# Chunked attention with a capacity-limited router: the first pair read with its zeros, one key chain for the last eight row tiles, other one-hot groups, earlier weights

## The chip, the core and the metric

The kernel runs on one NeuronCore of a Trainium2 chip. A core has five instruction streams that run side by side and meet in semaphores: TensorE (PE: matmuls; its weight loads are shown apart as PEld), VectorE (DVE), ScalarE (ACT), GpSimd (POOL) and SyncE (SP, which here only issues DMAs). Sixteen DMA engines move data between the chip's memory and the core's SBUF. They are fed from queues, of which three matter here: SP's, ACT's, and POOL's for gathers and scatters by index. The metric is device time in microseconds (us), the median over runs: 246.68 us for the kernel before (three runs, 246.67 to 246.94).

## What is computed

Attention in chunks of 64 positions is followed by a mixture of eight experts, of which each token uses the one with the largest logit, and each expert keeps at most `capacity` (80) tokens, those with the largest gate weights:

```python
scores = scale * q_c @ k_c.T                 # per chunk of 64, 8 x 8 heads x 9 chunks
attn = exp(scores - max); attn /= attn.sum() + 1e-09
x = (attn @ v_c) as [4608, 512]
logits = x @ w_gate                           # [4608, 8]
expert_idx = argmax(logits);  gate_w = softmax(logits)[expert_idx]
for e in range(8):
    tok = the (at most capacity) tokens of e with the largest gate_w
    out[tok] = gate_w[tok] * (relu(x[tok] @ w1[e]) @ w2[e])     # all other rows of out are 0
```

All data is float32: q, k and v of 8 x 8 heads x 576 x 64, w1 of 8 x 512 x 1024, w2 of 8 x 1024 x 512.

## The kernel before

**Pairs.** The attention runs over 18 pairs of row tiles (a row tile is 128 of the 4608 rows; 36 of them). Pair `n` needs its queries and keys in one of three buffers `qb` (`load_qk`, L320) and its values in one of three buffers `vb` (`load_v`, L328), each load in two DMAs of 64 partitions. In `qb` two of three column blocks are half zeros, so that one matmul makes the scores of two heads; those zeros are set once, at the start, by six DVE memsets (L637, L638), and the buffer's loads wait for them. `scores` (L338) fills PSUM, DVE subtracts the maxima (L348, L353), PE transposes (L363), ACT takes the exponential (L372), `values` (L391) multiplies with v, DVE divides (L406), `store` writes x to memory (`xs`, L419, L414), and PE transposes x for the router's logits (L443, L453). The loop is skewed: in turn `n` stand the scores of `n`, the transposes of x of `n-3`, the values of `n-2` and the exponentials of `n-1`. Every order here is written out by hand: each engine runs its instructions in the order of the code, and SP issues DMAs in the order of the code, each when its semaphores allow.

**Gate chains.** For each group of four row tiles `gate` computes level, one-hot of the expert (`mine`), the gate weight `g = 1 / sum` (L519, L521), the key (L483) and its split into three bfloat16 parts `comp` (L489 to L496) on POOL. Groups 28 and 32 come last, when all pairs are done.

**Routing.** `tally` counts on PE how many tokens lie above each of 256 levels, `left_add` (L568) and `threshold` (L574, L577, L580) find each expert's level, `mask` (L786) marks the candidates, a scan (L791) and three matmuls (L796) give each candidate its place, `ptok` (L802, L804). `hot` makes one-hot matrices of the places, 128 x 128 for each row tile, by DVE for several tiles at once (way "v", L588, at most HOT tiles in an instruction), by ACT (way "a", L598, L599) or by POOL (way "p", L601). 36 matmuls (L813) in the written order `order` collect the candidates' `comp` into `cand`. Then PE spreads the eight experts' keys (L848), DVE ranks them (L831, L837), PE places the chosen rows (L147), and POOL gathers their x from `xs` (L176). `keep_warm` (L610) issues matmuls of 256 columns whose result nobody reads.

**Experts.** Six blocks of 128 slots run layer 1 (L201) and layer 2 (L234). The weights come in 2 MB DMAs (L897) on SP's queue; those of experts 0 and 1 are cut into 16 pieces of 512 KB (`early_weights`, L629) and issued in the last turns by the table EARLY (keys 15 to 17 are loop turns, 18 to 21 places behind the loop). Some of them wait for a tiny POOL copy (L628) into the target tile. The later weights wait until the first gathers have landed (L896) or a buffer comes free; the rows of `out` that no token fills are cleared by DMAs from a zero tile (L616).

Of the kernel before, what the change touches and what calls it, by code (L numbers as in the profile page):

```python
# [8 lines left out]
F32 = mybir.dt.float32  # L9
BF16 = mybir.dt.bfloat16  # L10
# [25 lines left out]
LG = NT - 1  # L36
HOT = 8
OB = 171
LATER = [[(2, 1), (3, 0), (3, 1)], [(0, 2), (4, 0), (5, 0), (1, 2)], [(4, 1), (5, 1), (2, 2)], [(6, 0), (6, 1), (3, 2), (4, 2), (7, 0)], [(7, 1), (5, 2), (6, 2), (7, 2), (8, 2)], [], [], []]

EARLY = {15: [0], 16: [1, 2], 17: [3, 4], 18: [5, 6, 7], 19: [8, 9], 20: [10, 11], 21: [12, 13, 14, 15]}

# [11 lines left out]
@with_exitstack  # L54
def attention_moe(ctx: ExitStack, tc: tile.TileContext, qk, vv, wg, w1, w2, cap, cst, out):
    nc = tc.nc
# [224 lines left out]
    with ExitStack() as actx:  # L281
# [43 lines left out]

        def load_v(n):
            for h in range(2):
                nc.sync.dma_start(vbufs[n % NB][h:P:2, :, h],  # L328
                                  vv[n, :, h].rearrange("t p f -> p t f"))
# [126 lines left out]
        def gate(rt, n, lg, queue):  # L456
# [6 lines left out]
            def t2(nm):  # L463
                return gk.tile([P, n], F32, name=f"{nm}{rt}", tag=nm, bufs=3)
            sh, ex, wt, r = (t3(x) for x in ("sh", "ex", "wt", "r"))
            m, mw, sx, g, u8, lb = (t2(x) for x in ("gm", "mw", "sx", "gg", "u8", "lb"))
            bb = gk.tile([P, n], BF16, name=f"bb{rt}", tag="bb", bufs=3)
            kk, co = keys[:, sl, :], comp[:, sl]
            oh = mine[:, sl, :]
# [12 lines left out]
            def key():  # L482
                nc.gpsimd.tensor_tensor(kk, oh, g[:, :, None].to_broadcast(bc), op=ALU.mult)  # L483
                parts()

            def parts():
                p = nc.gpsimd
                for j, c0 in ((0, C_A), (1, C_B)):
                    p.tensor_tensor(  # L489
                        co[:, :, j, :], oh,  # L490
                        ct[:, c0 + rt:c0 + rt + n, None].to_broadcast(bc), op=ALU.mult)
                p.tensor_copy(co[:, :, 2, :], kk)
                p.tensor_tensor(r, kk, co[:, :, 2, :], op=ALU.subtract)
                p.tensor_copy(co[:, :, 3, :], r)
                p.tensor_tensor(r, r, co[:, :, 3, :], op=ALU.subtract)
                p.tensor_copy(co[:, :, 4, :], r)  # L496

            def level():
                with nc.allow_low_precision(reason="the same level is used everywhere"):
# [20 lines left out]
                        g, sx, 1e-9, None, op0=ALU.add)]  # L520
            late = [lambda: v.reciprocal(g, g), key]  # L521
            for fn in chain + ([] if rt >= 24 else rest + late):
# [59 lines left out]
        def hot(rt, way, n):  # L582

            if way == "v":
                if 'hot' not in S:
                    S['hot'] = wk.tile([P, 5, P, HOT], BF16, name="pk", tag="qb2", bufs=1), deque(range(5))
                oh = S['hot'][0][:, S['hot'][1].popleft()]
# [45 lines left out]
        with tc.manual_schedule():  # L633
            warm = gk.tile([P, 2 * P], BF16, name="warm", tag="lv", bufs=LV)
            nc.gpsimd.memset(warm, 0.0)
            for j, qb in enumerate(qbufs):
                nc.vector.memset(qb[:, :, 0:512], 0.0)  # L637
                nc.vector.memset(qb[:, :, 1024:1536], 0.0)  # L638
                if j == 0:
                    load_qk(0, (nc.sync, nc.scalar))  # L640
            nc.scalar.dma_start(ident, cst[:, C_ID:C_ID + P])
            for j, vb in enumerate(vbufs):
                (nc.vector, nc.gpsimd, nc.gpsimd)[j].memset(vb, 0.0)
            nc.vector.memset(wgp[:, :, 8:32], 0.0)
            pw = bank([P, 256])

# [9 lines left out]
            nc.scalar.mul(idp, ident, float(P))  # L656
            load_qk(1)
            load_qk(2)
            load_v(0)
            load_v(1)  # L660

            def late_constants():
# [106 lines left out]
            for j in range(33, 36):  # L769
                steps_(nc.vector, j)  # L770
            for k in EARLY[20]:
                early_weights(k, bo[:, 28:29])
            for k in EARLY[21]:
                early_weights(k, bo[:, 32:33])
            tally(28, 4)
            left_add(28)
            tally(32, 4)
            rest(28, "level", "sum")
            rest(32, "sum")
            rest(28, "inverse", "key")  # L780
            rest(32, "inverse", "key")
            keep_warm(1)
            threshold()
# [21 lines left out]
            cand = two[:, 1, 0:5 * NE].rearrange("p (c e) -> p c e", c=5)  # L805
            for rt, way in ((31, "p"), (32, "a"), (33, "a"), (34, "a"), (35, "p")):
                hot(rt, way, 1)
            for b0, n in ((0, 5), (5, 8), (13, 8), (21, 6), (27, 4)):
                hot(b0, "v", n)
            order = [*range(0, 13), 32, *range(13, 21), 33, 31, *range(21, 27), 34, 35,  # L810
                     *range(27, 31)]
            for j, rt in enumerate(order):
# [3 lines left out]
                    start=j == 0, stop=j == RT - 1)  # L816
                if rt in (4, 12, 20, 35):
                    keep_warm(1)
# [208 lines left out]
def _arrays(q, k, v, moe_w_gate, moe_w1, moe_w2, moe_capacity):  # L1027
# [7 lines left out]
    r["qk"] = np.ascontiguousarray(np.concatenate(  # L1035
        [np.where(f, k, q), np.where(f, q, k)], -1).reshape(NPAIR, 2, P, QK))
    r["vv"] = np.ascontiguousarray(t.reshape(NPAIR, 2, 2, 64, VW))
    r["wg"] = np.ascontiguousarray(moe_w_gate)
# [22 lines left out]
```

## Time and profile before

| | us |
|---|---|
| median of 3 runs | 246.68 |
| profiled execution | 246.04 |
| its span | 244.2 |
| PE busy | 224.2 (92%) |
| DVE / ACT / POOL busy | 119.1 / 65.8 / 56.6 |

The profile is of one execution, and its span is what its instructions cover. "Idle before, releaser" says how long an engine stood still ahead of an instruction and what ended that. PE's busy time contains the `keep_warm` matmuls, so a busy PE is not always one that the end waits for.

### The profile page before, as it was taken

The numbers are of one execution on the slowest core, as the hardware profiler recorded it, in microseconds if no ns is written. First come the engines' busy times: TensorE is split into PE (matmuls) and PEld (weight loads), VectorE is DVE, ScalarE is ACT, GpSimd is POOL, SyncE is SP. The second block draws the span as 40 slices with busy tenths as digits, with TensorE's granted clock in tenths as the row PEclk, the third lists the DMA queues.
The fourth block names the chain that finished last, engine by engine and source line by source line (L and its number), as shares of the span: only waits on it lengthen the run. The fifth ranks groups of instructions, "written<-read, shape, count | busy, mean of one in ns | idle before, by whom it ended". The sixth has DMA issues, their size and how long they took to land.

```text
span 244.2 us, 7221 instructions
## 1 busy us (share of the span) xinstructions
PE 224.2 (92%) x3121; PEld 143.5 (59%) x3121; DVE 119.1 (49%) x257; ACT 65.8 (27%) x115; POOL 56.6 (23%) x168
## 2 busy tenths in 40 slices
PE   8797799999999999989768979999999999999980
PEld 5587788898898989868547723434234223233320
DVE  7886668696968787877474721112111112111210
ACT  2013433372737364544622011202002002010000
POOL 8000300222222222328685370000000000000271
PEclk9999999999999999999987899999999999999998
DMA  4999999999999996889999979999999999999141
GB/s 127 407 359 337 411 409 406 407 408 404 389 370 349 374 359 219 293 293 300 280 410 410 366 213 400 401 395 415 414 400 409 416 409 415 403 400 403 71 164 61
DMA packets 34741, 84.71 MB, mean 347 GB/s; under 512 B 3024, under 2 KB 3152, under 8 KB 34704
## 3 DMA queue, kind: packets, MB, share of 16 engines
q1 hardware_dynamic: 33456, 80.72, 87.9%
q0 software_dynamic: 960, 2.88, 3.4%
q8 instruction: 26, 0.43, 0.7%
q10 hardware_dynamic: 288, 0.59, 0.6%
q14 instruction: 11, 0.09, 0.1%
HBM read 64.00 MB, written 20.45 MB: 346 GB/s over the span
## 4 chain that ended last, share of the span: by engine, by line
PE 70%; DMA 14%; SPq 5%; DVE 3%; POOL 3%; issue 2%; ACT 1%; POOLq 0%; DVEq 0%; ACTq 0%
PE o L391 13%; PE hc L201 13%; PE s L338 13%; PE yc L234 11%; DMA w<-in_w 7%; PE px L363 5%; DMA qb<-in_qk 5%; SPq L616 4%; PE pt L363 4%; PE small L443 4%; PE hpc L219 2%; DMA xgc<-xs,gic 2%; PE small L453 1%; PE pwarm L610 1%; PE xpc L189 1%
## 5 line engine op out<-in xcount | busy, mean ns | idle before, releaser
L201 PE MATMUL hc<-w,xtc 128*32 128x512 f32 x384 | 45.5, 594 | 0.5 <-ACT xtc L191 0.2
L234 PE MATMUL yc<-w,htc 128*32 128x512 f32 x384 | 42.3, 592 | 0.0
L338 PE MATMUL s<-qb 128*64 128x128 f32 x576 | 35.4, 276 | 4.4 <-DMA qb<-in_qk 3.2
L391 PE MATMUL o<-vb,pT 128*64 128x130 f32 x576 | 36.1, 276 | 0.0
L338 PEld LDWEIGHTS s<-qb 128*64 128x64 f32 x576 | 31.2, 137 | 7.2 <-DVE x L406 2.4
L391 PEld LDWEIGHTS o<-vb,pT 128*64 128x64 f32 x576 | 31.5, 135 | 1.2
L234 PEld LDWEIGHTS yc<-w,htc 128*32 128x32 f32 x384 | 12.4, 110 | 28.3 <-issue 28.3
L348 DVE TENSOR_REDUCE mx<-s 128x16 f32<-128x1024 f32 x18 | 22.0, 1225 | 14.1 <-PE s L338 14.0
L201 PEld LDWEIGHTS hc<-w,xtc 128*32 128x32 f32 x384 | 12.0, 110 | 28.2 <-issue 25.6
L372 ACT ACTIVATE pT<-pt 128x1024 f32<-128x1024 f32 x18 | 18.4, 1024 | 31.8 <-PE pt L363 31.8
L253 POOL DMA_INDIRECT out<-ysc,to x6 | 5.9, 991 | 86.6 <-SPq L912 84.4
L434 ACT COPY xT<-px 128x1024 f32<-128x1024 f32 x17 | 17.1, 1008 | 25.3 <-PE px L363 25.3
L406 DVE TENSOR_TENSOR x<-o,rc 128x1024 f32<-128x1024 f32 (+1 forms) x20 | 22.4, 1118 | 0.7
L353 DVE TENSOR_TENSOR sm<-s,mx 128x1024 f32<-128x1024 f32 x18 | 22.1, 1227 | 0.6
L206 ACT ACTIVATE hsc<-hc 128x512 f32<-128x512 f32 x6 | 3.6, 598 | 65.7 <-PE hc L201 65.7
L239 DVE TENSOR_SCALAR ysc<-yc,gatec 128x512 f32<-128x512 f32 x6 | 4.5, 752 | 33.5 <-PE yc L234 33.5
L223 DVE COPY htc<-hpc 128x512 f32<-128x512 f32 x6 | 4.2, 692 | 24.3 <-PE hpc L219 24.3
L208 DVE TENSOR_SCALAR hsc<-hc 128x512 f32<-128x512 f32 x6 | 4.1, 692 | 23.8 <-PE hc L201 23.8
L363 PE MATMUL pt<-ct,sm 64*128 64x64 f32 x288 | 12.8, 229 | 1.2 <-ACT pT L372 1.2
L363 PEld LDWEIGHTS pt<-ct,sm 64*128 64x128 f32 x288 | 10.4, 139 | 4.3 <-issue 2.8
L363 PE MATMUL px<-ct,x 64*128 64x64 f32 x288 | 12.8, 229 | 0.0
L533 ACT ACTIVATE lv<-io_b,bo 128x256 bf16<-128x256 bf16 x29 | 12.5, 498 | 0.4 <-DVE bo L514 0.4
(131 smaller groups left out, 216.5 us busy)
## 6 DMA issues: line engine op xcount, KB each, us to landing
w<-in_w SPq DMA_DIRECT2D x12, 2048.0 KB, 18.2
qb<-in_qk SPq DMA_DIRECT2D x35, 512.0 KB, 6.6
vb<-in_vv SPq DMA_DIRECT2D x36, 260.0 KB, 5.3
out<-zero SPq DMA_DIRECT2D x9, 1024.0 KB, 16.7
xs<-x SPq DMA_DIRECT2D x16, 512.0 KB, 6.2
w<-in_w SPq DMA_DIRECT2D x16, 512.0 KB, 7.1
xs<-x SPq DMA_DIRECT2D x4, 256.0 KB, 5.5
qb<-in_qk ACTq DMA_DIRECT2D x1, 512.0 KB, 4.3
```

What stands on the lines that cost most here:

```text
L201: nc.tensor.matmul(h[o:o + 32, :], lhsT=xT[r][:, b, o:o + 32], rhs=getw(groups[r][g])[0][:, b, 512 * f:512 * f + 512], start=(b == 0), sto ...
L234: nc.tensor.matmul(y[o:o + 32, :], lhsT=hT[r][c // 4][:, c % 4, o:o + 32], rhs=getw(groups[r][g])[1][:, c, :], start=(c == 0), stop=(c == ...
L338: nc.tensor.matmul(ps[64 * u:64 * u + 64, t, P * pr:P * pr + P].rearrange("p (h k) -> p h k", h=2), lhsT=t8[:, 1, pr, u, :], rhs=t8[:, 0:3 ...
L348: nc.vector.tensor_reduce(d['mx'], d['s8'], axis=AX.X, op=ALU.max)
L353: nc.vector.tensor_tensor(d['sm'].rearrange("p c k h -> p h c k"), d['s8'], d['mx'][:, :, :, None].to_broadcast([P, 2, 8, 64]), op=ALU.sub ...
L363: nc.tensor.transpose(pm[:, u, 64 * c:64 * c + 64], src(c)[rows], ident[rows, rows])
L372: nc.scalar.activation(d['pT'], pt, AF.Exp, scale=0.125)
L391: nc.tensor.matmul(po[64 * u:64 * u + 64, o:o + 130].rearrange("p (h x) -> p h x", h=2), lhsT=d['pT'][:, u, c:c + 64], rhs=v[:, :, pr, u, ...
L406: nc.vector.tensor_tensor(TT[T][:, r:r + nt, :].rearrange("p r (k h e) -> p (r k) h e", k=4, h=2), pov[..., 0:64], rc[:, :, :, None].to_br ...
L434: nc.scalar.copy(dst, pm)
L443: nc.tensor.matmul(pl[32 * j:32 * j + 32], lhsT=wgp[:, pr], rhs=xt[:, 4 * (j % 2) + pr, :], start=pr == 0, stop=pr == 3, tile_position=(0, ...
L533: nc.scalar.activation(lv, io_b, AF.Sign, bias=bo[:, rt:rt + 1], scale=-1.0)
```

## The change

The host lays out the first pair's queries and keys a second time with the zeros already in them (`qk0`, two blocks of 128 x 1536 float32); two DMAs, one of SP and one of ACT, read it with no memset ahead of them. Buffer 1's zeros stay on DVE, buffer 2's go to POOL, and the loads of pairs 1 and 2 and of values 0 and 1 are shared between SP's and ACT's queues. Groups 28 and 32 keep their sums in one tile `g8`, with one reciprocal and one key chain of eight row tiles where there were two of four. The DVE one-hots are made in three instructions (12, 12 and 6 row tiles) where there were five (5, 8, 8, 6 and 4); POOL makes those of 30 and 31, ACT those of 32 to 35. `keep_warm` calls move, and EARLY issues the pieces one place sooner, with two POOL copies in front of them where there were six.

```diff
@@ constants
-HOT = 8
+HOT = 12
-EARLY = {15: [0], 16: [1, 2], 17: [3, 4], 18: [5, 6, 7], 19: [8, 9], 20: [10, 11], 21: [12, 13, 14, 15]}
+EARLY = {15: [0, 1], 16: [2, 3], 17: [4, 5], 18: [6, 7, 8], 19: [9, 10, 11], 20: [12, 13], 21: [14, 15]}
@@ load_v
-        def load_v(n):
+        def load_v(n, engs=(nc.sync, nc.sync)):
             for h in range(2):
-                nc.sync.dma_start(vbufs[n % NB][h:P:2, :, h],
+                engs[h].dma_start(vbufs[n % NB][h:P:2, :, h],
@@ gate
-            m, mw, sx, g, u8, lb = (t2(x) for x in ("gm", "mw", "sx", "gg", "u8", "lb"))
+            m, mw, sx, u8, lb = (t2(x) for x in ("gm", "mw", "sx", "u8", "lb"))
+            if rt < 28:
+                g = t2("gg")
+            else:
+                if rt == 28:
+                    S['g8'] = gk.tile([P, 8], F32, name="g8", tag="g8", bufs=1)
+                g = S['g8'][:, rt - 28:rt - 24]
...
             def key():
-                nc.gpsimd.tensor_tensor(kk, oh, g[:, :, None].to_broadcast(bc), op=ALU.mult)
-                parts()
-
-            def parts():
-                p = nc.gpsimd
+                if rt == 32:
+                    keyed(28, 8, S['g8'], gk.tile([P, 8, NE], F32, name="r8", tag="r8", bufs=1))
+                elif rt < 28:
+                    keyed(rt, n, g, r)
+
+            def keyed(rt, n, g, r):
+                p, bc = nc.gpsimd, [P, n, NE]
+                kk, co, oh = keys[:, rt:rt + n], comp[:, rt:rt + n], mine[:, rt:rt + n]
+                p.tensor_tensor(kk, oh, g[:, :, None].to_broadcast(bc), op=ALU.mult)
...
-            late = [lambda: v.reciprocal(g, g), key]
+            late = [lambda: v.reciprocal(S['g8'] if rt == 32 else g, S['g8'] if rt == 32 else g)
+                    if rt != 28 else None, key]
@@ hot
-                    S['hot'] = wk.tile([P, 5, P, HOT], BF16, name="pk", tag="qb2", bufs=1), deque(range(5))
+                    S['hot'] = wk.tile([P, 3, P, HOT], BF16, name="pk", tag="qb2", bufs=1), deque(range(3))
@@ the start
-            for j, qb in enumerate(qbufs):
-                nc.vector.memset(qb[:, :, 0:512], 0.0)
-                nc.vector.memset(qb[:, :, 1024:1536], 0.0)
-                if j == 0:
-                    load_qk(0, (nc.sync, nc.scalar))
+            for t, eng in enumerate((nc.sync, nc.scalar)):
+                eng.dma_start(qbufs[0][:, t], qk0[t])
             nc.scalar.dma_start(ident, cst[:, C_ID:C_ID + P])
+            for j, eng in ((1, nc.vector), (2, nc.gpsimd)):
+                eng.memset(qbufs[j][:, :, 0:512], 0.0)
+                eng.memset(qbufs[j][:, :, 1024:1536], 0.0)
...
+            both = (nc.sync, nc.scalar)
+            load_qk(1, both)
+            load_qk(2, both)
+            load_v(0, both)
+            load_v(1, both)
...
-            load_qk(1)
-            load_qk(2)
-            load_v(0)
-            load_v(1)
@@ after the pairs
-            for k in EARLY[20]:
-                early_weights(k, bo[:, 28:29])
-            for k in EARLY[21]:
-                early_weights(k, bo[:, 32:33])
+            for j in (20, 21):
+                for k in EARLY[j]:
+                    early_weights(k, bo[:, 4 * j - 52:4 * j - 51] if k == EARLY[j][0] else None)
             tally(28, 4)
             left_add(28)
+            keep_warm(4)
             tally(32, 4)
             rest(28, "level", "sum")
             rest(32, "sum")
-            rest(28, "inverse", "key")
             rest(32, "inverse", "key")
-            keep_warm(1)
+            keep_warm(4)
             threshold()
...
-            for rt, way in ((31, "p"), (32, "a"), (33, "a"), (34, "a"), (35, "p")):
+            for rt, way in ((30, "p"), (31, "p"), (32, "a"), (33, "a"), (34, "a"), (35, "a")):
                 hot(rt, way, 1)
-            for b0, n in ((0, 5), (5, 8), (13, 8), (21, 6), (27, 4)):
+            for b0, n in ((0, 12), (12, 12), (24, 6)):
                 hot(b0, "v", n)
-            order = [*range(0, 13), 32, *range(13, 21), 33, 31, *range(21, 27), 34, 35,
-                     *range(27, 31)]
+            order = [*range(0, 12), 32, *range(12, 24), 33, 30, 34, *range(24, 30), 31, 35]
...
-                if rt in (4, 12, 20, 35):
+                if rt in (32, 34):
                     keep_warm(1)
@@ _arrays
+    a = r["qk"][0].reshape(2, 2, 64, QK)
+    z = np.zeros((2, 64, 2, QK + 512), a.dtype)
+    z[:, :, 0, :QK], z[:, :, 1, 512:] = a[:, 0], a[:, 1]
+    r["qk0"] = z.reshape(2, P, QK + 512)
```

On SP, at the start of the program, with what each row waits for (`qb_99` to `qb_101` are the three buffers of queries and keys, `vb_102` and `vb_103` two of values; DVE_49 and Pool_49 are semaphores of those engines, DMAHW those of DMAs). Before:

```order
L320 DMA qb_99<-in_qk 64x2x1024 [waits DVE_49]
L320 DMA qb_100<-in_qk 64x2x1024 [waits DVE_49] x2
L320 DMA qb_101<-in_qk 64x2x1024 [waits DVE_49] x2
L328 DMA vb_102<-in_vv 64x2x520 [waits DVE_49]
L328 DMA vb_102<-in_vv 64x2x520 [waits DMAHW0_49]
```

The same place on SP in the change:

```order
L647 DMA qb_99<-in_qk 128x1536
L320 DMA qb_100<-in_qk 64x2x1024 [waits DVE_49]
L320 DMA qb_101<-in_qk 64x2x1024 [waits Pool_49]
L328 DMA vb_102<-in_vv 64x2x520 [waits DVE_49]
L328 DMA vb_103<-in_vv 64x2x520 [waits DMAHW1_49,Pool_49]
```

The first load no longer waits for DVE and is half as large again; of each later pair one half stays on SP, and the other half stands on ACT.

On POOL, behind the key chain of group 24 (`gg` are the sums of a group, `w` targets of weights, `r` what a key has left after a part is taken off). Before, up to the middle of the second of two chains:

```order
L628 COPY w_1_2197<-bo 128x1 x2
L628 COPY w_1_2198<-bo 128x1 x4
L516 TENSOR_TENSOR kb<-mine,bb_2212 128x4x8
L519 TENSOR_SCALAR gg_2209<-sx_2208 128x4
L519 TENSOR_SCALAR gg_2276<-sx_2275 128x4
L483 TENSOR_TENSOR keys<-mine,gg_2209 128x32
L489 TENSOR_TENSOR comp<-mine,ct 128x4x8 x2
L492 CAST comp<-keys 128x4x8
L493 TENSOR_TENSOR r_2205<-keys,comp 128x32
L494 CAST comp<-r_2205 128x4x8
L495 TENSOR_TENSOR r_2205<-r_2205,comp 128x32
L496 CAST comp<-r_2205 128x4x8
```

The same place on POOL in the change:

```order
L638 COPY w_1_2140<-bo 128x1 x2
L525 TENSOR_TENSOR kb<-mine,bb_2212 128x4x8
L528 TENSOR_SCALAR g_2211<-sx_2208 128x4
L528 TENSOR_SCALAR g_2211<-sx_2275 128x4
L496 TENSOR_TENSOR keys<-mine,g_2211 128x64
L498 TENSOR_TENSOR comp<-mine,ct 128x8x8 x2
L501 CAST comp<-keys 128x8x8
L502 TENSOR_TENSOR r_2368<-keys,comp 128x64
L503 CAST comp<-r_2368 128x8x8
L504 TENSOR_TENSOR r_2368<-r_2368,comp 128x64
L505 CAST comp<-r_2368 128x8x8
L611 TENSOR_SCALAR pk_2415<-ct,ptok 128x128
```

Four copies and the second chain of eight instructions are gone, the one chain is twice as wide, and POOL's first one-hot stands right behind it.

## Rows read from the trace of the kernel before

**Rows 1.** The page, the chain that ended last, by engine

```profile
PE 70%; DMA 14%; SPq 5%; DVE 3%; POOL 3%; issue 2%; ACT 1%; POOLq 0%; DVEq 0%; ACTq 0%
```

**Rows 2.** Timeline of the start: start us, length us, engine, line, operation [idle before <-releaser]

```profile
1.00 0.91 DVE L637 MEMSET qb<- 128x1024 f32 x1 [1.00 <-PEq L1050]
1.94 5.97 SPq L320 DMA_DIRECT2D qb<-in_qk  x5
...
7.49 1.97 PE L338 MATMUL s<-qb 128*64 128x128 f32 x32 [0.98 <-DMA qb<-in_qk]
```

**Rows 3.** Windows at the start: stretch, length, busy us by engine, PEclk, DMA share, GB/s

```profile
6.00:7.00 1.00, 0.52 (x3) 0.12 (x1) 0.84 (x2) 0.00 (x0) 0.00 (x0) 1.00 1.04 415
14.00:15.00 1.00, 1.00 (x22) 1.00 (x20) 0.73 (x1) 0.00 (x0) 0.00 (x0) 1.00 0.92 280
```

**Rows 4.** Loads of `qb` for pair 4: count, issue ns, first and last issue, landing

```profile
L320 SPq DMA_DIRECT2D qb<-in_qk x2: 602/604/605, 17.7 to 18.3; - x2
DMA to landing us min/median/max: 6.0/6.7/7.5
```

**Rows 5.** Timeline, scores of pair 4

```profile
25.97 1.97 PE L338 MATMUL s<-qb 128*64 128x128 f32 x32 [1.25 <-DVE x L406]
```

**Rows 6.** Timeline, from the last levels to the threshold

```profile
122.66 0.70 POOL L628 COPY w<-bo 128x1 f32<-128x1 f32 x4 [0.54 <-DVE bo L514]
...
123.70 0.27 PE L610 MATMUL pwarm<-io_b,ones_b 128*128 128x256 bf16 x1
...
123.96 0.48 DVE L521 RECIPROCAL gg<-gg 128x4 f32<-128x4 f32 x2 [0.57 <-POOL gg L519]
...
124.57 0.19 PE L577 MATMUL small<-ge,ones_b 128*128 128x8 bf16 x2 [0.60 <-DVE ge L574]
```

**Rows 7.** Timeline, POOL: a cast alone, one beside the one-hots, the last two one-hots

```profile
120.38 0.21 POOL L492 CAST comp<-keys 128x32 bf16<-128x32 f32 x1
...
128.85 0.69 POOL L494 CAST comp<-r 128x32 bf16<-128x32 f32 x1
...
130.65 1.20 POOL L601 TENSOR_SCALAR pk<-ct,ptok 128x128 bf16<-128x128 f32 x2
```

**Rows 8.** Timeline, DVE's one-hots, PE's wait among the 36 matmuls, and their end

```profile
127.23 3.37 DVE L588 TENSOR_TENSOR pk<-io_h,ptok_b 128x640 bf16<-128x640 bf16 x5
...
130.72 0.68 PE L813 MATMUL two<-comp,pk 128*128 128x40 bf16 x9 [0.85 <-POOL comp L496]
...
132.47 0.18 DVE L823 TENSOR_REDUCE kc<-two 128x8 f32<-128x24 f32 x1 [1.87 <-PE two L813]
```

**Rows 9.** Timeline of DVE in two short stretches: one-hots by width

```profile
127.88 1.59 DVE L588 TENSOR_TENSOR pk<-io_h,ptok_b 128x1024 bf16<-128x1024 bf16 x2
...
130.01 0.60 DVE L588 TENSOR_TENSOR pk<-io_h,ptok_b 128x512 bf16<-128x512 bf16 x1
```

**Rows 10.** Windows in the routing, columns as in rows 3

```profile
127.50:128.00 0.50, 0.50 (x5) 0.32 (x4) 0.50 (x2) 0.47 (x2) 0.49 (x1) 0.50 0.98 401
...
134.00:135.00 1.00, 1.00 (x7) 0.81 (x6) 0.66 (x5) 0.00 (x0) 0.00 (x0) 0.50 1.05 426
```

**Rows 11.** Timeline, from the spread keys to the first places

```profile
132.81 1.92 PE L848 MATMUL kr<-ct,kc 128*128 128x128 f32 x8
...
136.22 0.19 PE L147 MATMUL small<-cb,sel 128*32 128x5 bf16 x4
136.34 2.14 PE L610 MATMUL pwarm<-io_b,ones_b 128*128 128x256 bf16 x18
```

**Rows 12.** The chain that ended last, in order of time: the first gather

```profile
136.92 4.68 DMA xgc<-xs,gic
```

**Rows 13.** The six gathers' time to landing

```profile
DMA to landing us min/median/max: 3.4/5.9/7.6
```

**Rows 14.** Expert 2's first weights: count, issue ns, issue time, landing

```profile
L897 SPq DMA_DIRECT2D w<-in_w x1: 368/368/368, 127.0 to 127.0; - x1
DMA to landing us min/median/max: 14.2/14.2/14.2
```

More of the change, by code (lines that the diff above doesn't have):

```diff
@@ L54, in attention_moe @@
 @with_exitstack
-def attention_moe(ctx: ExitStack, tc: tile.TileContext, qk, vv, wg, w1, w2, cap, cst, out):
+def attention_moe(ctx: ExitStack, tc: tile.TileContext, qk, qk0, vv, wg, w1, w2, cap, cst, out):
     nc = tc.nc
@@ L465, in gate @@
             sh, ex, wt, r = (t3(x) for x in ("sh", "ex", "wt", "r"))
-            m, mw, sx, g, u8, lb = (t2(x) for x in ("gm", "mw", "sx", "gg", "u8", "lb"))
+            m, mw, sx, u8, lb = (t2(x) for x in ("gm", "mw", "sx", "u8", "lb"))
[5 more added lines that the diff above has]
+                g = S['g8'][:, rt - 28:rt - 24]
             bb = gk.tile([P, n], BF16, name=f"bb{rt}", tag="bb", bufs=3)
-            kk, co = keys[:, sl, :], comp[:, sl]
             oh = mine[:, sl, :]
```

## The prediction

> **What bounds the kernel now.** I read the page's chain of waits first, then the timeline where that chain leaves TensorE, then the windows for clock and DMA. The chain is TensorE for 70% and DMA for 14% [rows 1]: pairs and experts are TensorE work almost without a gap, so the change can only move what stands in front of them. There are two such places.
>
> The start. Four engines are free at about 1.00, but SP's first load goes out at 1.94, when DVE has set the first zeros, and the first scores run at 7.49 [rows 2]. That wait is not the one that counts. From about 4 us on the DMA engines have no pause (share 1.04 and 0.92 in the two windows), at 415 GB/s on queries and keys and 280 GB/s where the shorter rows of v are moved [rows 3]. The second half of pair 4's load, issued at 18.3, lands 7.5 later, at 25.8 [rows 4], and the scores of pair 4 start at 25.97 [rows 5]. The row names DVE as the releaser, but the landing and DVE's end fall together there, and no later scores wait for their data. So the start ends with that load, and it is a matter of bytes behind the first DMA.
>
> The routing. From the last attention matmul to the first gather everything is a chain over small instructions. TensorE waits 0.85 among its 36 one-hot matmuls for POOL's second key chain and goes on at 130.72; the collected keys are read at 132.47 [rows 8]. From there to the first places (136.22) it takes 3.75 with TensorE granted 0.50, its 1.2 GHz level, for most of it [rows 10, 11]. The gather issued at 136.92 lands 4.68 later, at 141.60 [rows 12], and frees both the experts' matmuls and the later weights, so that what is won up to there moves the whole expert stage, its short waits for weights with it.
>
> **The change part by part.** All times are those of the profiled execution, 246.04 in all (span 244.2); the median is 246.68, 0.64 more, which I add at the end.
>
> *A, the start.* First issue at 1.00 instead of 1.94: -0.94. The zeros now come through the DMA engines: 2 x 128 rows x 512 x 4 B = 0.524 MB more, at 415 GB/s 1.26, at 280 GB/s 1.87. Both apply to the landing of pair 4's load, since the engines are full in between: +0.32, with bounds of -0.94 (the bytes cost nothing) and +0.93. I take +0.3, as these are rows of queries and keys like those of the first window. Sharing the loads between two queues and the freed DVE memsets (four left of six, two of them on POOL) I cost at nothing: the DMA queue is their cover, and TensorE waits for bytes either way. The larger table for DVE's one-hots is one longer POOL copy in a stretch in which POOL stands idle.
>
> *B, POOL copies.* The four copies of 122.66 take 0.70, 0.175 each; one of them is left, so the level product and the two sums behind them come 0.53 sooner. DVE's reciprocal waited for those sums (0.57), ran twice in 0.48, and held the instruction behind it, which releases TensorE at 124.57 [rows 6]. One reciprocal is saved, some 0.24. But four `keep_warm` matmuls now stand where one stood, about 0.12 each [rows 11], behind the counts, from 123.70 on [rows 6], so TensorE is free only near 124.15: I take -0.4 for the threshold and all that DVE does after it (bounds 0 and -0.77). The four `keep_warm` between the two counts fit into TensorE's wait for DVE there.
>
> *C, one-hots and the key chain.* DVE made 31 tiles in 3.37 [rows 8]. A width of 1024 took 0.80 and one of 512 0.60 [rows 9], so 1536 should take 1.0 and 768 0.7; two and one of these are 2.7, and some 2.5 as neighbours overlap. They start at 127.23 - 0.4 = 126.83 and end near 129.35. POOL now has eight instructions of double width instead of sixteen. A cast of 32 elements took 0.21 and a one-hot of 128 0.60 [rows 7], so 64 elements should take 0.34 and, with the gaps, a chain some 3.0. It starts at 124.1, behind the reciprocal; mask and scan on DVE hold it for about 0.5, so some two or three instructions are left when the one-hots begin. Beside those a cast took 0.69 instead of 0.21, 0.48 more [rows 7]: three at 0.82 end near 129.3, where the second chain ended at 130.65. TensorE, which by then has done its first twelve matmuls, goes on at about 129.5 instead of 130.72. Left are 24 matmuls and two warm ones where there were 23 and two, 1.8 as before: the keys are read at 131.3, -1.15 (B is in it). POOL's one-hots of 30 and 31 come at 129.9 and 130.5 and are wanted at 130.5 and 131.0; ACT's four are done before 130. Bounds: -0.3 if the chain takes twice the time that I give it, -2.0 if DVE doesn't hold it and the second one-hots end the wait.
>
> *D, the clock.* The 3.75 are 0.34 up to the spread keys, 1.92 for these, and 1.49 in which 8 warm matmuls hold TensorE. At full clock 18 of those took 2.14 [rows 11], so 8 take 0.95, and the spread keys about 1.0: 2.3, or 2.5 with DVE's ranks, which are then the limit. The fall to 0.50 came twice, each time after a stretch in which TensorE stood still or had only matmuls of 8 or 40 columns. The change puts seven more `keep_warm` matmuls ahead of the first fall and halves the wait ahead of the second. If the clock stays at 2.4 GHz from the collected keys on, the first places follow them by 2.5 and not 3.75: -1.25. Bounds 0 and -1.25; I take -1.25. The gather then goes out at 136.92 - 2.4 = 134.5.
>
> *E, the gather among the weights.* It meets more of the stream now. Expert 2's first 2 MB, issued at 127.0, landed at 141.2 [rows 14]; the first gather, which ran into the end of that, took 4.68 [rows 12]; the six took 3.4 at best, with the queues empty, and 7.6 at worst, in the full stream [rows 13]. Issuing one piece of 0.524 MB earlier ends that stream 1.3 to 1.9 sooner, not 2.4. In the last pairs the piece stands ahead of a load of v that TensorE needs two turns later, so there it costs nothing; if that cover is gone, it costs at most its own 1.3 to 1.9. I take 5.3 for the gather: it lands at 139.8, -1.8 against 141.60. Bounds: 137.9 and 142.1.
>
> Sum: -1.8 + 0.3 = -1.5; 246.04 - 1.5 = 244.5 in the profiled execution, 245.2 as a median.
>
> The Trainium skill would price E otherwise ("DMA: Bandwidth & Descriptors", section on queues, rings and completion order): each DMA engine takes packets from its queues in turn. By that a gather of 256 KB would be slowed by no more than its own size again, about 0.6 at 415 GB/s, to 4.0, and would land at 138.5. The 7.6 of the fourth gather speaks against it, but two other gathers stood before that one in the same queue.
>
> **The rivals.**
> 1. The gather shares the DMA engines evenly: 4.0 and not 5.3, landing at 138.5, -3.1 with all else as above and +0.3 for the start: 243.9. For it: the first gather started its packets inside the stream and was only 1.3 over the best. Against: up to 7.6 for the later ones. 15%.
> 2. The clock stays low: `keep_warm` has the count, but the 36 small matmuls still bring 40 columns each, and the next stretch falls to 1.2 GHz as before. Then D is nothing, the gather goes out at 135.75 and takes 5.0: 140.75, -0.85, +0.3: 246.1. For it: the second fall came with TensorE busy most of the stretch. 20%.
> 3. The end on the other side: the early gather is swallowed by the weights. It decides where the stream of expert 2 outlasts the gather's packets: then the gather takes 7.6 as the fourth did, 134.5 + 7.6 = 142.1, +0.5, and with +0.3 at the start the kernel is slower: 247.5. Against: the pieces issued sooner shorten the stream, and its last part before was nearly empty. 10%.
> 4. The start costs the full +0.93, because the long rows move no faster than v's: 245.8. For it: nothing in the rows but the 280. 8%.
>
> **How the numbers follow.** My forecast has 44%, the rivals 15, 20, 10 and 8%; 3% are left for what I have not seen. Range: rival 1 and rival 2 are taken in, rival 3 is left out: 243.6 to 246.9. Within 0.2% (0.5 us, about what a measurement of this kernel tells from no change) lie 246.2 to 247.2. Rival 2 sits on that edge; I count a bit more than half of it as faster. Faster: 0.76; the same: 0.13; slower: 0.11.
>
> **What would show it.** In the profile after: SP's and ACT's first loads at about 1.0, the scores of pair 4 at 26.2 to 26.4, no gap later in the pairs; the threshold's matmuls 0.4 nearer to the pairs' end; one POOL chain ending near 129.6; granted clock 1.00 through the spread keys, and the first places 2.5 behind the collected keys; the gather landing near 140.1; the expert stage as long as before. I am wrong if pair 4's scores move by more than 0.9 either way, if TensorE waits for POOL beyond 130.7, or if the gather takes over 7 us.

## The result, and the profile after

The changed kernel takes 243.94 us (median of 5 runs, 243.01 to 245.05); the kernel before took 246.94 beside it. The ratio is 0.988, with a 95% interval of 0.984 to 0.992: 3.0 us faster, 1.9 to 3.9. I had forecast 245.2, so the sign is right and the gain half of what came. The profiled execution took 243.36 (span 241.6, before 244.2). On its way to those 2.6 us nearly every term moved by more than I gave it.

The start, as in [rows 2], [rows 4] and [rows 5], timeline of the kernel after (start, length, engine, line, operation, idle time and releaser):

```profile
0.72 0.40 SPq L647 DMA_DIRECT2D qb<-in_qk  x1
...
11.12 1.97 PE L338 MATMUL s<-qb 128*64 128x128 f32 x32 [2.19 <-DMA qb<-in_qk]
...
24.35 1.97 PE L338 MATMUL s<-qb 128*64 128x128 f32 x32
```

The scores of pair 4 start at 24.35 and wait for no data; before it was 25.97. The pairs end 1.62 sooner. Windows of the same kernel, to set beside [rows 3], show a part of why: SP's first load no longer waits for VectorE, and from 14 to 15 the DMA engines now reach 418 GB/s and not 280.

```profile
6.00:7.00 1.00, 0.64 (x5) 0.16 (x3) 0.00 (x0) 0.00 (x0) 1.00 (x4) 1.00 1.02 394
14.00:15.00 1.00, 1.00 (x13) 0.75 (x12) 0.96 (x2) 0.80 (x1) 0.00 (x0) 1.00 1.07 418
```

The routing, which answers to [rows 6 to 9], [rows 11] and [rows 12], all engines, in order of time:

```profile
122.12 0.20 DVE L530 RECIPROCAL g<-g 128x8 f32<-128x8 f32 x1 [0.34 <-POOL g L528]
122.40 0.30 POOL L496 TENSOR_TENSOR keys<-mine,g 128x64 f32<-128x64 bf16 x1 [0.32 <-DVE g L530]
122.51 0.20 PE L587 MATMUL small<-ge,ones_b 128*128 128x8 bf16 x2
...
125.17 0.24 POOL L505 CAST comp<-r 128x64 bf16<-128x64 f32 x1
125.29 2.42 DVE L598 TENSOR_TENSOR pk<-io_h,ptok_b 128x1536 bf16<-128x1536 bf16 x3
125.61 2.54 POOL L611 TENSOR_SCALAR pk<-ct,ptok 128x128 bf16<-128x128 f32 x2 [0.21 <-ACT ptok L813]
...
128.71 0.18 DVE L831 TENSOR_REDUCE kc<-two 128x8 f32<-128x24 f32 x1 [1.00 <-PE two L821]
128.95 1.08 PE L856 MATMUL kr<-ct,kc 128*128 128x128 f32 x8
...
130.84 0.20 PE L147 MATMUL small<-cb,sel 128*32 128x5 bf16 x4
...
138.97 1.09 PE L189 MATMUL xpc<-ct,xgc 128*128 128x128 f32 x4 [4.00 <-DMA xgc<-xs,gic]
140.09 5.17 PE L201 MATMUL hc<-w,xtc 128*32 128x512 f32 x32
```

GpSimd's one chain of keys ends at 125.41, 0.12 after VectorE's one-hots have begun, and TensorE never waits for it. The collected keys are read at 128.71, 3.76 sooner; the first places stand 2.13 behind them, where it was 3.75. So the first gather goes out at 131.53 and not at 136.92. But of these 5.39 us the chain that ended last gives back half in one row:

```profile
131.53 7.30 DMA xgc<-xs,gic
```

It took 4.68 before [rows 12]. It lands at 138.83, 2.77 sooner than before, and TensorE has stood still for 4.00. In that wait its granted clock falls to 0.50, the 1.2 GHz level:

```profile
123.00:124.00 1.00, 1.00 (x7) 0.71 (x5) 0.97 (x2) 0.00 (x0) 0.92 (x3) 0.50 1.02 401
130.00:131.00 1.00, 1.00 (x14) 0.71 (x12) 1.00 (x8) 0.00 (x0) 0.00 (x0) 1.00 1.07 418
136.00:137.00 1.00, 0.00 (x0) 0.00 (x0) 0.50 (x2) 0.00 (x0) 0.70 (x2) 0.70 0.99 373
138.00:139.00 1.00, 0.03 (x1) 0.06 (x1) 0.14 (x1) 0.00 (x0) 0.83 (x1) 0.50 0.77 229
```

The first matmuls of layer 1 (hc, L201) then take 5.17, where before they took 3.64, and stand 1.12 behind the start of the transposes (xpc, L189) and not 0.87: 1.78 lost, so that the matmuls behind them are only 0.99 ahead of before. The rest comes near the end. Waits of TensorE and of its weight loads (PEld) from 137 to 238 in the kernel before (engine, line, what was waited for, us in total, times, longest); the kernel after has none:

```profile
PEld hc L201 <- DMA w<-in_w: 2.1, 2, 1.1
PE hc L201 <- DMA w<-in_w: 0.2, 1, 0.2
```

The last matmuls of layer 2 (yc, L234) start 3.11 sooner (226.51, 223.40): 0.99 and 2.12 of these stalls. The last scatter of results into `out` takes 0.5 longer to land and gives that back. That is the 2.6 of the span.

### The profile page after: what moved, and what is told of

It is laid out like the page before. It is cut to its first block, busy times and chain, and to the rows that moved or that the text cites. A ratio compares the mean times of both kernels' runs of the same rounds, so it can differ in the third digit from the quotient of the medians.

```text
span 241.6 us, 7213 instructions
## 1 busy us (share of the span) xinstructions
PE 222.9 (92%) x3126; PEld 143.5 (59%) x3126; DVE 114.8 (48%) x250; ACT 66.6 (28%) x117; POOL 56.6 (23%) x158
## 4 chain that ended last, share of the span: by engine, by line
PE 85%; DMA 6%; DVE 4%; issue 1%; ACT 1%; POOL 0%; POOLq 0%; DVEq 0%; ACTq 0%
PE hc L201 18%; PE yc L234 17%; PE o L391 14%; PE s L338 13%; PE px L363 5%; PE pt L363 5%; PE small L443 4%; DMA qb<-in_qk 3%; DMA xgc<-xs,gic 3%; PE hpc L219 3%; PE pwarm L620 2%; PE xpc L189 1%; PE small L453 1%; PE small L563 1%; PE two L821 1%
## 5 line engine op out<-in xcount | busy, mean ns | idle before, releaser
L201 PE MATMUL hc<-w,xtc 128*32 128x512 f32 x384 | 45.1, 611 | 0.0
L234 PE MATMUL yc<-w,htc 128*32 128x512 f32 x384 | 42.3, 592 | 0.0
L234 PEld LDWEIGHTS yc<-w,htc 128*32 128x32 f32 x384 | 12.4, 110 | 28.3 <-issue 28.3
L201 PEld LDWEIGHTS hc<-w,xtc 128*32 128x32 f32 x384 | 12.7, 112 | 26.8 <-issue 25.1
```

The costliest lines, as they stand in the source:

```text
L201: nc.tensor.matmul(h[o:o + 32, :], lhsT=xT[r][:, b, o:o + 32], rhs=getw(groups[r][g])[0][:, b, 512 * f:512 * f + 512], start=(b == 0), sto ...
L234: nc.tensor.matmul(y[o:o + 32, :], lhsT=hT[r][c // 4][:, c % 4, o:o + 32], rhs=getw(groups[r][g])[1][:, c, :], start=(c == 0), stop=(c == ...
```

## Experiments

What was open: where the start's 1.6 come from, which edit freed the routing, why the gather got longer, and whether any of it reaches the end. My theory was that the gather stands behind the stream of weights, and that the start is the only gain. The kernel before scattered from 244.5 to 250.0 on the chips used here, so a ratio has an interval of 0.3 to 1% and the mechanisms are read from the profiled executions. "Pairs' end" is the start of the last gate matmuls (L443): 118.71 before, 117.09 after.

### The start: s1, s2, s3, s4, s5

s1_start_only is the kernel before with the new start; s2_old_start is the changed kernel with the old one:

```diff
-            for t, eng in enumerate((nc.sync, nc.scalar)):
-                eng.dma_start(qbufs[0][:, t], qk0[t])
+            for j, qb in enumerate(qbufs):
+                nc.vector.memset(qb[:, :, 0:512], 0.0)
+                nc.vector.memset(qb[:, :, 1024:1536], 0.0)
+                if j == 0:
+                    load_qk(0, (nc.sync, nc.scalar))
...
-            load_qk(1, both)
...
+            load_qk(1)
```

> The kernel before with the new start alone (first pair with its zeros from memory, loads of the first pairs on two queues). Theory: the start is a gain by itself: scores of pair 4 near 24.4 instead of 25.97, all pairs 1.6 sooner, and the weights go out with the pairs, so the gather (4.7) keeps its length and the end moves by the same 1.6: 245.1 against 246.7. Rival: the pairs end sooner but the first gather ends with expert 2's weights wherever it starts, so little of it is left: 246.2 or more.

> The changed kernel with the start of the kernel before; routing and weights stay new. Theory: scores of pair 4 back near 26.0, pairs' end 1.6 later (last small count at 118.7), the routing behind it as in the changed kernel, first gather issued at about 133.1 and again 7.3 long: 1.6 over the changed kernel, 245.5. Rival (the gather ends with the weights, which follow the pairs only in part): 244.3.

s1: 245.95, ratio 0.999 (0.995 to 1.003): the rival's size, but for a reason neither named. TensorE waits 2.35 for pair 1 and its clock falls, so the scores of pair 1 take 3.52 and the pairs end at 118.94, no sooner than before:

```profile
11.43 3.52 PE L338 MATMUL s<-qb 128*64 128x128 f32 x32 [2.35 <-DMA qb<-in_qk]
```

s2: 245.41, ratio 0.996 (0.992 to 1.001). Scores of pair 4 at 25.23, pairs' end at 117.97, gather out at 132.35, 7.50 long. The start's gain is thus 0.9 in this pair of executions; the same old start gave 25.97 in one and 25.23 in another, so it varies by 0.7 from run to run.

s3_one_queue and s5_start_one_queue take the sharing out again, from the changed kernel and from s1:

```diff
-            both = (nc.sync, nc.scalar)
+            both = (nc.sync, nc.sync)
```

> The changed kernel, with the loads of pairs 1 and 2 and of the first two v on SP's queue alone. Theory: sharing two queues is what keeps short rows of v from slowing the DMA engines, so the dips to 280 to 340 GB/s return and the scores of pair 4 come near 25.3 instead of 24.35, total 0.5 to 1.0 over the changed kernel. Rival: only the earlier first load counts; scores of pair 4 stay within 0.3 of 24.35 and the total stays.

> The kernel before with the new start, its first loads on SP's queue alone. Theory: early issue alone makes the gain of the start, and on one queue pair 1's keys land in time, so TensorE's clock doesn't fall in the start as it did with two queues: scores of pair 4 at 24.5, pairs' end at 117.1, gather landing about 1.6 sooner than before (140.0) and total 1.2 to 1.8 under before. Rival (the start is no gain of its own): pairs end sooner, the total stays within 0.4 of before.

s3: 243.35, ratio 0.986 (0.975 to 0.997); its rival holds. Pair 1's scores start at 9.80 and not at 11.12, pair 4's within 0.1 of the changed kernel:

```profile
9.80 1.97 PE L338 MATMUL s<-qb 128*64 128x128 f32 x32 [0.90 <-DMA qb<-in_qk]
...
24.45 1.97 PE L338 MATMUL s<-qb 128*64 128x128 f32 x32 [0.19 <-DMA qb<-in_qk]
```

So the second queue gains nothing that shows and makes pair 1 wait. s5: 244.79, ratio 0.991 (0.988 to 0.994): with one queue the new start alone is worth 1.4 to 2.9 us, pairs' end at 116.97. But its gather, out at 133.58 instead of 136.92, takes 6.91, and the profiled span is only 0.9 under before.

s4_zeros_set loads the first pair as before, with VectorE setting its zeros, and keeps the rest of the new start:

```diff
-                eng.dma_start(qbufs[0][:, t], qk0[t])
...
+            for j, eng in ((0, nc.vector), (1, nc.vector), (2, nc.gpsimd)):
+                eng.memset(qbufs[j][:, :, 0:512], 0.0)
+                eng.memset(qbufs[j][:, :, 1024:1536], 0.0)
+                if j == 0:
+                    load_qk(0, (nc.sync, nc.scalar))
```

> The changed kernel, with the first pair loaded as before (zeros set by VectorE, no zeros from memory), everything else of the new start kept. Theory: the first load goes out 1.2 later but brings 0.52 MB less (1.26 at 415 GB/s): scores of pair 4 within 0.3 of 24.35 and the total within 0.3 of the changed kernel. Rival: the bytes are hidden and the earlier issue counts: scores of pair 4 near 25.5, total 1.2 over the changed kernel.

246.04, ratio 0.996 (0.991 to 1.000). That is nearer to the rival, 1.2 over the changed kernel, than to my theory. But the profiled execution has the slow clock in the start too (scores of pair 1 at 12.87 take 3.68, after a wait of 3.50), so it doesn't tell what the zeros from memory are worth by themselves. That stays open.

### The routing: r2, r3

r2_two_chains makes the last eight row tiles' keys in two chains again, r3_fewer_warm takes the added warm matmuls away:

```diff
-                if rt == 32:
-                    keyed(28, 8, S['g8'], gk.tile([P, 8, NE], F32, name="r8", tag="r8", bufs=1))
...
+            rest(28, "inverse", "key")
             rest(32, "inverse", "key")
--- r3_fewer_warm
-            keep_warm(4)
             tally(32, 4)
...
-            keep_warm(4)
+            keep_warm(1)
             threshold()
```

> The changed kernel with the keys of the last eight row tiles in two chains again (sixteen small GpSimd instructions and two reciprocals instead of eight and one). Theory: a small GpSimd instruction costs nearly the same at 32 and 64 elements, so this adds some 8 x 0.26 = 2.1 of GpSimd time, more beside VectorE's one-hots: TensorE waits for GpSimd again among the 36 one-hot matmuls and the collected keys come 1.5 to 2.5 later behind the pairs' end. Rival: the chains are covered and the keys come within 0.4.

> The changed kernel with the warm matmuls of the kernel before around the last counts (none instead of four between the counts, one instead of four ahead of the threshold). My prediction's theory: these keep the clock up, so without them it falls again and the spread keys take 1.9 instead of 1.08, the first places 3.4 or more behind the collected keys instead of 2.13. Rival: the clock fell at 122.5 in spite of them and is back at 1.00 by 126.5 because the one-hots' matmuls now run without a wait and wide enough in time, so the spread keys stay at 1.08 and the places at 2.1 behind them.

r2: 243.97, ratio 0.990 (0.984 to 0.996). Timeline of its TensorE:

```profile
130.02 0.18 PE L812 MATMUL two<-comp,pk 128*128 128x40 bf16 x1 [1.46 <-POOL comp L496]
...
131.85 1.94 PE L847 MATMUL kr<-ct,kc 128*128 128x128 f32 x8
...
135.41 0.19 PE L147 MATMUL small<-cb,sel 128*32 128x5 bf16 x4
...
140.46 0.63 PE L189 MATMUL xpc<-ct,xgc 128*128 128x128 f32 x4 [0.92 <-DVE flag_i L875]
141.33 3.64 PE L201 MATMUL hc<-w,xtc 128*32 128x512 f32 x32 [0.24 <-ACT xtc L191]
```

The wait for GpSimd is back (1.46), the keys come 12.9 behind the pairs' end instead of 11.6, the clock is low again (1.94) and the places follow at 3.8: together 3.0 us later than in the changed kernel, 136.11 for the gather. And the experts end their first hc at 145.0, against 145.3, though r2's pairs had ended 1.6 later (its start had the slow clock): nothing of those 3.0 us reaches them. The later gather took at most 4.4 us and left no long wait in which the clock falls.

r3: 243.44, ratio 0.989 (0.985 to 0.993), the rival's outcome:

```profile
129.13 1.08 PE L855 MATMUL kr<-ct,kc 128*128 128x128 f32 x8
```

The seven warm matmuls do nothing for it here. The spread keys ran at low clock in two of the four profiles with two chains (before, r2) and in none of the ten with one. In the other two of the four, s1 and s5, TensorE waits 1.2 for GpSimd as well and the spread still takes 1.08. So it may be that the wait makes the fall possible and one chain takes it away; two of four against none of ten doesn't prove it, and what decides it in a run is open. No run changes the one-hot groups alone.

### The gather: r1, e1, e2

r1_weights_later puts the pieces of the weights back to their old places, e1_hold_w2 lets expert 2's first 2 MB wait for the first gather, e2_warm34 fills TensorE's wait:

```diff
-EARLY = {15: [0, 1], 16: [2, 3], 17: [4, 5], 18: [6, 7, 8], 19: [9, 10, 11], 20: [12, 13], 21: [14, 15]}
+EARLY = {15: [0], 16: [1, 2], 17: [3, 4], 18: [5, 6, 7], 19: [8, 9], 20: [10, 11], 21: [12, 13, 14, 15]}
--- e1_hold_w2
-LATER = [[(2, 1), (3, 0), (3, 1)],
+LATER = [[(2, 0), (2, 1), (3, 0), (3, 1)],
...
-            part(2, 0)
--- e2_warm34
             nc.tensor.matmul(pt, lhsT=ones_b, rhs=inc[:, :, RT - 1], start=True, stop=True)
+            keep_warm(34)
```

> The changed kernel with the weights at their old places (a piece later), routing and start stay new. Theory, from the runs so far: the first gather lands some 15 behind the issue of expert 2's first 2 MB wherever the gather itself goes out (14.1 to 15.8 in eight runs), so what sets the experts' start is when the weights are out. The old places put that issue back to 8 to 9 behind the pairs' end instead of 6.4; the gather goes out at the same 14.4 behind it, takes 9 or more, and lands 2 later; total 1 to 2 over the changed kernel. Rival (my prediction's): a piece earlier or later hardly counts and the gather takes 7.3 or a bit more: within 0.4 of the changed kernel.

> The changed kernel; the first 2 MB of expert 2's weights wait for the first gather, like the later ones. Theory: that stream is what the gather stands behind (it landed at 138.84, the stream at 139.2), so without it the gather takes 3.5 to 4.2 instead of 7.30, TensorE waits 1.0 or less and its clock stays at 1.00 (first hc 3.64 instead of 5.17): the experts begin 3.2 to 4.7 sooner. The later weights then start some 3 later against the experts; up to 1.3 of stalls come back. Total 240.5 to 242.5 against 243.9. Rival: the gather is long for a reason of its own and still takes 6.5 or more; then the total is 243.9 or above.

> The changed kernel with 34 more warm matmuls on TensorE while it waits for the first gather. Theory: the wait of 4.00 let the clock fall to 0.50, which costs the first hc 5.17 - 3.64 = 1.5 and the transposes 0.25: with the wait filled the first hc takes 3.64, total -1.6 to -1.8, 242.2. Rival: the fall has another cause, or the warm matmuls run past the landing: total within 0.4 of the changed kernel.

r1: 244.04, ratio 0.991 (0.987 to 0.994), profiled span 241.6, that of the changed kernel. Expert 2's first weights went out 2.2 later, as expected, the gather landed 0.35 later:

```profile
125.72 17.38 SPq L905 DMA_DIRECT2D w<-in_w  x4
```

```profile
131.97 7.21 DMA xgc<-xs,gic
```

My theory's rule, landing 15 behind that issue, falls (here 13.5), and with it the idea that the moved pieces won something. The weights themselves landed 2.7 later (141.75, in the changed kernel 139.01), so the gather doesn't simply end with them. What it does wait for shows in the single DMA packets of the traces: the gather's first one starts 2.0 behind the gather's issue in before, r2, e1, b1 and b2, and 3.3 to 4.5 behind it in all the others, where the stream is still full. In the changed kernel it is 3.9; the DMA queues from 131.5 to 135.4 (packets, MB, share of the 16 engines' time) show only SP's stream and one other packet, and none of the gathers' queue:

```profile
q1 hardware_dynamic: 405, 1.63, 101.8%
q8 instruction: 1, 0.02, 1.6%
```

Of the 2.62 that this gather took longer than before, 1.9 lie ahead of its first packet and 0.7 behind it.

e1: 247.56, ratio 1.003 (0.999 to 1.008). The gather goes out at 133.30, is in by 137.84 (4.5 at most), TensorE keeps its clock and the first hc takes 3.64: half of the theory. The other half, the price, was far too low. TensorE's waits for weights in the expert stage:

```profile
PE hc L201 <- DMA w<-in_w: 4.3, 2, 3.1
PEld hc L201 <- DMA w<-in_w: 4.0, 1, 4.0
```

The experts begin 3.1 nearer to the pairs' end, and their last yc starts 5.0 later than in the changed kernel; its pairs had ended 1.8 later.

e2: 246.35, ratio 0.996 (0.991 to 1.001). Timeline of TensorE and ScalarE:

```profile
138.77 0.63 PE L189 MATMUL xpc<-ct,xgc 128*128 128x128 f32 x4
...
141.77 0.65 ACT L191 COPY xtc<-xpc 128x256 f32<-128x256 f32 x2 [12.45 <-remote]
...
142.19 5.34 PE L201 MATMUL hc<-w,xtc 128*32 128x512 f32 x32 [2.80 <-ACT xtc L191]
```

The clock did stay up to the transposes (0.63 and not 1.09), but ScalarE's copy of them came some 2.4 behind their end, for a reason the profile calls remote, and behind this new wait the clock fell after all. The 1.6 that I expected didn't come, and the kernel is no faster than the changed one; what the filled wait is worth by itself, and why ScalarE was late, is open.

### What binds the end: b1, b2

b1_half_held (on s3's start) holds only the second half of those 2 MB, and lets the next weights wait for the first gather alone; b2_clear_early also moves one of the nine 1 MB stores of zeros from the expert stage to pair 14's turn, where the DMA engines have room:

```diff
+                if r == 0:
+                    part(2, 0, xg[0][:, 0:1], (2, 4))
...
-                        part(e, l, xg[e - 2][:, 0:1] if r == 0 else None)
+                        part(e, l, xg[0][:, 0:1] if r == 0 else None)
...
-            part(2, 0)
+            part(2, 0, None, (0, 2))
--- b2_clear_early, beyond b1_half_held
-[(0, 2), (4, 0), (5, 0), (1, 2)]
+[(4, 0), (5, 0), (1, 2)]
...
+                if n == 14:
+                    clear(0)
```

> The changed kernel with the first loads on one queue; the second half of expert 2's first weights waits for the first gather, and all of the next weights wait for the first gather instead of the first, second and third. Theory: 1 MB less in front of the gather brings its landing 2.5 sooner (5.0 instead of 7.30 long), TensorE waits under 2 and keeps its clock (first hc 3.64), and the DMA engines have no half-empty stretch of 5 us behind it, so the later weights are not later: experts begin 2.5 to 4 sooner, total 241.0 to 242.5. Rival: the whole expert stage is bound by the bytes of the weights, so an earlier first gather only brings waits for weights back: total 243 to 244.

> The kernel of b1_half_held with one of the nine 1 MB stores of zeros to the output (the first) moved from the expert stage into the turn of pair 14, where the DMA engines were 0.60 to 0.64 busy from 91 to 97. Theory: the expert stage is bound by the bytes of its DMA traffic, 1 MB at 410 GB/s is 2.5 us; without it the later weights land 2.5 sooner, the wait of 3.08 for weights near 195 falls to 0.6 or goes, the pairs' end stays at 117.0, total 2 to 2.5 under b1_half_held (240.5 to 241.2). Rival: the wait at 195 hangs on when weight buffers come free and not on bytes: it stays at 2.5 or more and the total within 0.5 of b1_half_held.

b1: 243.19, ratio 0.987 (0.983 to 0.991). The gather is in before it is asked for, the first hc runs from 137.18 in 3.64, and the experts are 4.4 ahead of the changed kernel. Then the rival holds, near 195:

```profile
137.18 3.64 PE L201 MATMUL hc<-w,xtc 128*32 128x512 f32 x32 [0.24 <-ACT xtc L191]
...
194.89 3.63 PE L201 MATMUL hc<-w,xtc 128*32 128x512 f32 x28 [3.08 <-DMA w<-in_w]
```

b2: 240.45 (239.66 to 240.85), ratio 0.977 (0.973 to 0.981), span 238.4. The same place, and the stretch that took the moved megabyte, in b1 and then in b2:

```profile
91.00:97.00 6.00, 6.00 (x117) 5.37 (x117) 5.45 (x11) 3.55 (x7) 1.59 (x8) 1.00 0.62 208
```

```profile
91.00:97.00 6.00, 6.00 (x115) 5.34 (x113) 5.31 (x11) 3.34 (x6) 1.65 (x8) 1.00 1.00 370
...
192.50 3.63 PE L201 MATMUL hc<-w,xtc 128*32 128x512 f32 x28 [0.30 <-DMA w<-in_w]
```

1 MB out of the expert stage takes 2.78 off the wait and 2.5 off the span, what 1 MB costs at 410 GB/s. So the wait of b1 hangs on bytes: once the experts begin as early as there, the stage is bound by what it has to move. In the changed kernel TensorE waits for no weights behind the first gather, and moving the store there alone was not tried. b2_clear_early is the fastest kernel of the study, 2.3% under the kernel before.

## Why the prediction was right in sign and half in size

**A, the start: the step that failed.** I took +0.3 and it was -1.62, beyond my lower bound of -0.94; my own mark (0.9 either way) was passed. Two terms of that step failed. One is "First issue at 1.00 instead of 1.94: -0.94". The loads go out at 0.72, and in the first 5 us the DMA engines move 213 GB/s on average where it was 64: 0.75 MB more, 1.8 us at 415 GB/s. The other is the rate behind it, which I had taken from [rows 3]: from 5 to 24 us it is 398 GB/s and not 370, 0.53 MB more, 1.3 us. Against these stand the 0.52 MB of zeros, the 1.3 that I had priced. That makes -1.8, and the second half of pair 4's load does land 1.8 sooner (25.83, 24.04). That the sharing costs nothing was right (s3). Windows before and then after:

```profile
0.00:5.00 5.00, 3.91 (x19) 2.79 (x20) 3.51 (x4) 0.59 (x1) 4.47 (x9) 1.00 0.31 64
5.00:24.00 19.00, 15.85 (x256) 13.74 (x254) 15.12 (x16) 4.25 (x6) 0.59 (x3) 1.00 1.02 370
```

```profile
0.00:5.00 5.00, 3.91 (x19) 2.73 (x20) 3.45 (x3) 0.00 (x0) 4.47 (x9) 1.00 0.60 213
5.00:24.00 19.00, 16.23 (x264) 13.99 (x264) 11.81 (x14) 4.85 (x6) 2.38 (x5) 1.00 1.03 398
```

I took the rate of a stretch for a property of the rows in it. It is none: from 12 to 13, where v's rows are most of what is moved, the kernel before reached 395 GB/s too. Why the rate rose is open. The three profiles with the old first load have 370 to 379 GB/s from 5 to 24 us, the eleven with the new one 392 to 399; but the number of loads under way doesn't explain the 280 (at 14 us six before and eight after). A part of the 1.62 is the one execution of the kernel before: against s2, with the same old start, it is 0.9.

**B, the threshold:** forecast -0.4, and -0.44 came (2.06 in all, of which 1.62 is the start).

**C, the chain of keys:** forecast -1.15, came -2.14 behind the pairs' end, past my -2.0. The chain's 3.0 us were right (122.40 to 125.41). But they held VectorE's mask and scan already, and I then let three instructions wait once more beside the one-hots. r2 shows what the one chain was worth between these two profiles: 1.3 in the keys and 1.7 in the clock behind them.

**D, the clock:** -1.25, and -1.62 came; the reason was the wrong one of the two that I gave. Without the added warm matmuls the spread keys take the same 1.08 (r3), and the clock did fall ahead of the one-hots in spite of them. What the changed kernel lacks is the wait for GpSimd; and since s1 and s5 kept their clock with that wait, the 1.62 hangs in part on the luck of the profile before.

**E, the gather:** 5.3, and 7.30 came, over the 7 that I had named as a sign of being wrong. The price is rival 3's, the landing is not, since the gather went out 3 earlier than I had it. I had set one gather's time and added a little; in fact it takes 6.5 to 7.5 where most of the stream is still ahead of it (the changed kernel, s1 to s5, r1, r3) and 5.0 or less where it is issued into the stream's end or the stream is cut (before, r2, e1, b1, b2). Of the time won ahead of it, 2.6 went into its length. Rival 1, by which the gather would take 4.0, doesn't fit these rows; 243.9, its time, was met for other reasons.

The Trainium skill ("DMA: Bandwidth & Descriptors", section "Queues, rings and completion order") has each DMA engine take turns between queues, but it counts a turn as a whole packet of about 9 to 17 descriptors (more than a packet of the traces, which is one row), which the prediction left out. If each 4 KB row of the stream, 0.16 us in the trace, is one descriptor, a turn of the stream would hold the gather for 1.4 to 2.7, an estimate. The extra 1.3 to 2.5 ahead of the gather's first packet would agree with that; no run here tests it.

**What no term held.** Two effects on the experts, of opposite sign: the 4.00 of idle TensorE cost 1.78 through the clock, and the weights' stalls of 2.1 went. I had written "the expert stage as long as before". The weights behind the first gather wait for it, so their stream moves with its landing (-2.77) and TensorE's work only by 0.99: the stream is 1.8 further ahead of TensorE, which fits the stalls that went.

Summed: start -1.62, threshold -0.44, keys -1.70, clock -1.62 make -5.38 at the gather's issue; gather +2.62, clock +1.78, stalls -2.12, last scatter +0.5: -2.6. My sum got to -1.5 by errors that partly cancelled. Of the terms in it the start's was 1.9 too high and the gather's 2.0 too low; the two effects on the experts were not in it. The forecast lay in its range, but its story of where the time is won was wrong: in r2 the routing gives 3.0 us away and the total doesn't show it.

How the 3.0 us divide among the edits is not settled: the new start on one queue was worth 1.4 to 2.9 by itself, the new routing and weights with the old start up to 2.0, the parts don't add, and the intervals overlap.

## What to carry to other kernels

Before you price what comes ahead of a transfer, ask what it queues behind: here a gather issued 5.4 us sooner landed 2.8 sooner, because it waited behind the same stream of weights. When compute and DMA are both over 90% busy in a stage, look for bytes in it that could go elsewhere; in b2 one megabyte moved into a half-empty stretch gave 2.5 us of the span, about as much as the whole change (2.6). A load that waits for a memset also delays all loads behind it: in the first 5 us of the kernel before, 0.75 MB less was moved.

## What the runs showed of the hardware

Halving the number of small GpSimd instructions by doubling their width was nearly pure gain: alone, they took 0.24 to 0.31 for 64 elements and 0.21 to 0.29 for 32. GpSimd's one-hots of 128 took 1.27 each beside VectorE's (2.54 for two above) and 0.60 after them [rows 7]. Loads spread over two queues in turn made the first of them land later (pair 1's scores at 11.12, with one queue at 9.80) and no later scores sooner by more than 0.1. A gather issued while SP's stream was full had its first packet 3.3 to 4.5 us after its issue, and 2.0 where the stream ran out in time. And a wait of 2.2 to 2.4 us for data in the start sometimes cost TensorE its clock (s1: scores of 3.52) and sometimes not (the changed kernel: 1.97); with it the pairs end 1.6 to 1.9 later.
